# One scatter a unit instead of two, and folds kept out of the units that split rows

## The chip, the cores and the metric

The kernel runs on one core of a Trainium2 chip. The metric is the device time of one execution in microseconds (us). The engines are named as in the profile: PE is TensorE, DVE is VectorE, ACT is ScalarE, POOL is GpSimd, SP is SyncE, which here issues transfers. PEld is PE's loading of weights, which runs beside its products.

## The reference, cut to what matters

```python
X = np.fft.fft(np.fft.fft(x, axis=1), axis=2).real   # x: 8 x 3072 x 256
x = X.reshape(24576, 256)
x = (x @ w_a) * (x @ w_b) @ w_out                    # 256 -> 1536 -> 256
logits = x @ w_gate                                  # 8 experts
e_idx = argmax(logits)
gate_w = softmax(logits)[e_idx]
eom = sigmoid(x @ w_output_gate)
for e in range(8):                                   # tokens of expert e only
    out[mask] = gate_w * eom[e] * (relu(x[mask] @ w1[e]) @ w2[e])
```

## The kernel before, in words

Numbers are carried as pairs of fp16, a high and a low half, so one fp32 product becomes three fp16 ones. The program has two parts. In the first, up to about 1990 us, the transform, the first block of products and the gate are computed, and each token's row is written to an area of DRAM that is sorted by expert. In the second, the experts' products run over that area. The change touches the first part alone.

The first part is a list of 327 units (`plan`), which every engine runs through in the same order. A tile is 1024 tokens, 3 for each of the 8 batches (0 to 23), and takes 12 units, f 0 to 11. In each of them PE makes 12 products of 128x512 (line 828, into `s`) and 24 of 128x256 (line 894, into `y`), for one unit behind. Between them DVE makes five passes over `s` (lines 835 to 840 for the unit before, 861 for this one, into `EE`). The second half of PE's line 828 needs line 861's two results. Line 840 ends a unit's share on DVE; then ACT makes the high half of the result `hl` (line 845) and POOL the low half (line 847, "the subtraction" from here on). Units of a second kind, nine before tiles 6, 12 and 18, hold the transform's products.

Beside this chain every unit takes up pieces of other work, and a planner places them. `deal` goes through a list of items, each with a least distance to the one before and a cost for each engine, and moves an item to the next unit until the unit's `BUDGET` and a budget over three units (`THREE`) hold. A piece for "pool0" is put ahead of the unit's subtraction on POOL, one for "pool" or "dve" behind the unit's own work. The pieces that the change and the prediction speak of:

- `post_items(T)`, after a tile: squares, then the rows in two halves, on ACT (`row_hi`) and on DVE (`row_lo`, line 947, "low halves" from here on: 2, 3 and 3 of them in three units, which are f 4, 5 and 6 of the next tile), transposes issued by SP (`turn`), the gate (`gate0` to `gate3`), the place in the sorted area (`place`) and last eight scatters (line 1050), which POOL issues as indirect transfers and which each wait for the landing of the one before.
- `fold_items(b)`, for the batches ahead: six chunks c, each with a first piece (`fold1`, lines 519 to 521) and a second (`fold2`, lines 529 to 532, and for c of 3 to 5 lines 534 and 535 too), on POOL; SP loads and places rows beside them.
- `expert_items(e)`: the experts' weights are split into halves, the low ones on DVE (lines 412 and 465).

```python
t.append((1 + (i == 0 and k == 0), [("pool", 2.1 if k == 0 else 3.6 if c > 2 else 2.2, fn)] + nx + due))
```

Of the kernel before, what the change touches and what calls it, by code (L numbers as in the profile page):

```python
# [13 lines left out]
ALU = mybir.AluOpType  # L14
# [4 lines left out]
B, S, D = 8, 3072, 256  # L19
# [15 lines left out]
NTILE = 3 * B  # L35
# [6 lines left out]
def chain_kernel(ctx, tc, x, x384, w_a, w_b, w_out, w_gate, w_og, w1, w2, dft, c16, c32, ids, out):  # L42
    nc = tc.nc
    w_a, w_b, w_out = (w.bitcast(I32).rearrange("a (b c) -> a b c", c=2) for w in (w_a, w_b, w_out))
    pe, act, dve, pool, sp = nc.tensor, nc.scalar, nc.vector, nc.gpsimd, nc.sync
# [12 lines left out]
    def place_at(off, dtype, shape, spec, **kw):  # L58
        size = 4 if dtype in (FP32, I32) else 2
        n = 1  # L60
        for k in shape:
            n *= k
        v = big[:, off // 2:off // 2 + n * size // 2]
        if dtype != FP16:
            v = v.bitcast(dtype)
        return v.rearrange(spec, **kw) if spec else v
# [5 lines left out]
    F32 = place_at(24576, FP32, [6, 2, D], "p (a b c) -> p a b c", a=6, b=2)  # L72
# [99 lines left out]
    def run(point):  # L172
# [1 line left out]
            fn()  # L174

    BUDGET = {
        "B": {"act": 2.8, "dve": 1.75, "pool": 3.6, "pe": 1.0, "sp": 4.0},
        "D": {"act": 1.8, "dve": 1.8, "pool": 3.2, "pe": 1.0, "sp": 4.0},
    }
    THREE = {"act": 6.5, "dve": 5.0, "pool": 9.0}  # L180

# [316 lines left out]
    def fold_items(b, eng):  # L498
        st = {}
# [15 lines left out]
        def fold1(c):  # L515
            def go():
                P = st["P", c]
                Q = place_at(Qo, FP32, [4, D], "p (a b) -> p a b", a=4)
                eng.tensor_tensor(out=Q[:, :, 0:128], in0=P[:, :, 0:128], in1=P[:, :, 128:256], op=ALU.add)
                eng.tensor_tensor(out=Q[:, :, 129:256], in0=P[:, :, 0:127], in1=P[:, :, 128:255], op=ALU.subtract)  # L520
                eng.tensor_copy(out=Q[:, :, 128:129], in_=P[:, :, 256:257])
            return go

        def fold2(c):
            def go():
                P = st.pop(("P", c))
                Qv = place_at(Qo, FP32, [4, D], "p (h j d) -> p h j d", h=2, j=2)
                A, T = P[:, 0:2, 0:256], P[:, 2, 0:256]
                eng.tensor_tensor(out=A[:, :, 0:129], in0=Qv[:, :, 0, 0:129], in1=Qv[:, :, 1, 0:129], op=ALU.add)
                eng.tensor_tensor(out=A[:, :, 129:256], in0=Qv[:, :, 0, 129:256], in1=Qv[:, :, 1, 129:256], op=ALU.subtract)  # L530
                eng.tensor_tensor(out=T if c > 2 else F32[:, c, 0, :], in0=A[:, 0, :], in1=A[:, 1, :], op=ALU.add)
                eng.tensor_tensor(out=F32[:, c, 1, :], in0=A[:, 0, :], in1=A[:, 1, :], op=ALU.subtract)
                if c > 2:
                    eng.tensor_tensor(out=F32[:, c, 0, :], in0=F32[:, c - 3, 0, :], in1=T, op=ALU.subtract)
                    eng.tensor_tensor(out=F32[:, c - 3, 0, :], in0=F32[:, c - 3, 0, :], in1=T, op=ALU.add)
            return go

        def norm(c):
# [64 lines left out]
        t = [(0, [("sp", 1, load(0))])]  # L603
        norms = deque()
        for i, c in enumerate(order):
            for k, fn in enumerate((fold1(c), fold2(c))):
                if i == 1 and k == 0:
                    t.append((0, [("sp", 1, load384)]))
                due = [norms.popleft()] if i > 3 and norms else []
                nx = [("sp", 1, load(order[i + 1]))] if k == 1 and i < 5 else []  # L610
                t.append((1 + (i == 0 and k == 0), [("pool", 2.1 if k == 0 else 3.6 if c > 2 else 2.2, fn)] + nx + due))
            if i == 1:
                t.append((1, [("sp", 1, place384)]))
            if c > 2:
                norms += [("act", 0.6, norm(c - 3)), ("act", 0.6, norm(c))]
# [285 lines left out]
    def post_items(T):  # L901
        t, j0, nj = T
        ns = 1 if t == NTILE else 2
        nt = nj * ns
        st = {}
# [142 lines left out]
        def scatter(w):  # L1048
            def go():
                pool.indirect_dma_start(out=rows, out_offset=bass.IndirectOffsetOnAxis(ap=st["di"][:, w:w + 1], axis=0), in_=rowit[:, w, :], in_offset=None, bounds_check=ROWS - 1, oob_is_err=False)  # L1050
            return go

        def c(fn, a, b):
            return fn(min(a, nt), min(b, nt))

        k = nt / 8
        items = [
        ]
# [3 lines left out]
        last = None  # L1062
        for a, b in ((0, 2), (2, 5), (5, 8)):
            if a >= nt:
                continue
            m = min(b, nt) - a
            items.append((0 if last is None and nt > 4 else 1, [("act", 0.4 * m, c(row_hi, a, b)), ("dve", 0.38 * m, c(row_lo, a, b))] + ([("sp", 2, last)] if last else [])))
            last = c(turn, a, b)
        items += [
            (1, [("sp", 2, last), ("dve", 0.4, gate0)]),  # L1070
# [2 lines left out]
            (1, [("act", 0.25, exp2), ("dve", 0.8, gate3)]),  # L1073
            (0, [("pe", 1, place_pe), ("act", 0.25, place_copy), ("dve", 1.1, place)]),
        ]
        for w in range(0, nt, 2):
            items.append((1, [("pool0", 1.3, scatter(w))] + ([("pool", 1.3, scatter(w + 1))] if w + 1 < nt else [])))
        return items

# [134 lines left out]
    for u, un in enumerate(plan):  # L1214
        if un[0] == "D":
            first_of.setdefault(un[1], u)
            if pending:
                T, f = pending.pop(0)
                if f == NF - 1:
                    ends[T] = u  # L1220
        else:
            begins.setdefault(un[1], u)
            pending.append((un[1], un[2]))
            if len(pending) > 3:
                T, f = pending.pop(0)
# [28 lines left out]
    with tc.manual_schedule():  # L1254
# [167 lines left out]
        for T in tiles:  # L1422
            t, j0, _ = T
# [52 lines left out]
        items, late_early, weigh = early_items()  # L1476
# [8 lines left out]
        for u, un in enumerate(plan):  # L1485
            if un[0] == "D":
                _, g, i, k, n = un
# [363 lines left out]
```

## Time and profile before

| | |
|---|---|
| Median of three runs | 3059.37 us (3047.44 to 3063.09) |
| Profiled execution | 3057.12 us, of which the profile's span is 3055.4 us |
| PE | 2881.0 us busy, 94% of the span |
| DVE, POOL, ACT | 2209.5, 1335.7, 1315.1 us busy |
| Mean granted clock of PE | 0.976 |

PE's share is so high that time can be lost only where PE stands still or has the lower clock; the idle time of the other engines matters where PE waits for them.

### The profile page before, as it was taken

The numbers are of one execution on the slowest core, as the hardware profiler recorded it, in microseconds if no ns is written. First come the engines' busy times: TensorE is split into PE (matmuls) and PEld (weight loads), VectorE is DVE, ScalarE is ACT, GpSimd is POOL, SyncE is SP. The second block draws the span as 40 slices with busy tenths as digits, with TensorE's granted clock in tenths as the row PEclk, the third lists the DMA queues.
The fourth block names the chain that finished last, engine by engine and source line by source line (L and its number), as shares of the span: only waits on it lengthen the run. The fifth ranks groups of instructions, "written<-read, shape, count | busy, mean of one in ns | idle before, by whom it ended". The sixth has DMA issues, their size and how long they took to land.

```text
span 3055.4 us, 62396 instructions
## 1 busy us (share of the span) xinstructions
PE 2881.0 (94%) x24101; PEld 2184.9 (72%) x24101; DVE 2209.5 (72%) x4079; ACT 1315.1 (43%) x2605; POOL 1335.7 (44%) x1083
## 2 busy tenths in 40 slices
PE   6899899989999989999989999989999999999998
PEld 4466666656666756666666666678888888888898
DVE  8779699688999688999777998744555555555556
ACT  4454455545455445455444454432333333333332
POOL 6466587365775455775333445413211111111112
PEclk7899999999999999999999999999999999999999
DMA  5421722541221541221452212363222222222211
GB/s 190 118 60 43 177 74 60 145 107 40 77 76 47 137 116 46 77 72 46 99 126 84 77 50 82 87 186 98 58 51 51 50 53 52 51 53 51 51 44 35
DMA packets 363577, 244.48 MB, mean 80 GB/s; under 512 B 303101, under 2 KB 320669, under 8 KB 362382
## 3 DMA queue, kind: packets, MB, share of 16 engines
q1 hardware_dynamic: 342158, 184.75, 24.5%
q0 software_dynamic: 18816, 51.54, 4.9%
q10 hardware_dynamic: 2304, 4.20, 0.5%
q8 instruction: 188, 3.08, 0.4%
q14 instruction: 111, 0.91, 0.1%
HBM read 106.60 MB, written 70.33 MB: 58 GB/s over the span
## 4 chain that ended last, share of the span: by engine, by line
PE 75%; DVE 11%; issue 7%; DMA 3%; ACT 2%; POOL 0%; SPq 0%; DVEq 0%; POOLq 0%; ACTq 0%
PE s L828 19%; PE y L894 18%; PE g L1598 16%; PE g L1622 15%; PE s L662 3%; DVE EE L861 2%; DVE s L837 2%; DVE rows L947 1%; DVE hf L840 1%; DMA big<-in_dft_dram 1%; DVE AM L835 1%; DMA rows<-rows,di 1%; PE s L962 1%; ACT BP L834 1%; PE s L289 1%
## 5 line engine op out<-in xcount | busy, mean ns | idle before, releaser
L828 PE MATMUL s<-big 128*128 128x512 f16 x3456 | 824.9, 389 | 74.1 <-DVE EE L861 66.8
L847 POOL TENSOR_TENSOR hl<-hf,hl 128x1024 f16<-128x1024 f32 x288 | 626.4, 2175 | 566.2 <-ACT hl L845 422.9
L894 PE MATMUL y<-big,hl 128*128 128x256 f16 x6912 | 821.6, 273 | 1.0 <-POOL hl L847 1.0
L894 PEld LDWEIGHTS <-hl 128*128 128x128 f16 x6912 | 672.8, 98 | 152.0 <-issue 12.2
L828 PEld LDWEIGHTS <-big 128*128 128x128 f16 x3456 | 344.2, 100 | 448.4 <-issue 118.2
L1625 POOL DMA_INDIRECT out_dram<-o,di x189 | 195.4, 1034 | 777.3 <-ACT o L1624 524.8
L845 ACT ACTIVATE hl<-hf 128x1024 f16<-128x1024 f32 x288 | 303.8, 1055 | 499.2 <-DVE hf L840 434.3
L1598 PE MATMUL g<-yt,w1t 128*128 128x256 f16 (+1 forms) x4704 | 492.8, 265 | 3.5 <-DVE w1t L1579 3.5
L1622 PE MATMUL g<-w2t,hh 128*128 128x256 f16 x2896 | 479.5, 273 | 0.0
L1598 PEld LDWEIGHTS <-w1t 128*128 128x128 f16 x4704 | 432.0, 98 | 50.1 <-DVE w1t L1579 3.8
L1601 DVE SCALAR_TENSOR_TENSOR hl<-g,hh 128x512 f16<-128x512 f32 x378 | 260.3, 691 | 240.8 <-ACT hh L1600 239.9
L1622 PE MATMUL g<-w2t,hl 128*128 128x256 f16 x1448 | 394.7, 273 | 0.0
L1600 ACT ACTIVATE hh<-g 128x512 f16<-128x512 f32 x378 | 225.3, 598 | 276.3 <-PE g L1598 276.3
L1622 PEld LDWEIGHTS <-hh 128*128 128x128 f16 x3024 | 295.0, 98 | 33.7
L1050 POOL DMA_INDIRECT rows<-rows,di x192 | 191.7, 998 | 264.4 <-DMA rows<-rows,di 199.2
L836 DVE SCALAR_TENSOR_TENSOR hf<-s,BP 128x512 f32<-128x512 f32 x288 | 198.3, 688 | 112.9 <-ACT BP L834 102.7
L1583 DVE COPY w2t<-big 128x4104 f16 x98 | 120.5, 1229 | 206.7 <-PE g L1622 206.7
L1624 ACT ACTIVATE o<-g,sc 128x256 f32<-128x256 f32 x189 | 89.7, 474 | 409.6 <-PE g L1622 360.5
L835 DVE SCALAR_TENSOR_TENSOR AM<-EE,s 128x512 f32<-128x512 f32 x288 | 195.9, 680 | 30.7 <-PE s L828 28.3
L861 DVE SCALAR_TENSOR_TENSOR EE<-big,w,s 128x512 f32<-128x512 f32 x288 | 201.5, 741 | 0.0
L861 DVE SCALAR_TENSOR_TENSOR EE<-xe,w,s 128x512 f32<-128x512 f32 x288 | 201.4, 740 | 0.0
L834 ACT ACTIVATE BP<-s 128x512 f32<-128x512 f32 x288 | 170.2, 591 | 67.6 <-PE s L828 64.3
(332 smaller groups left out, 3039.5 us busy)
## 6 DMA issues: line engine op xcount, KB each, us to landing
big<-in_x_dram SPq DMA_DIRECT2D x48, 514.0 KB
big<-in_dft_dram SPq DMA_DIRECT2D x60, 384.0 KB
big<-in_moe_w_dram SPq DMA_DIRECT2D x16, 1024.0 KB
wsc<-big SPq DMA_DIRECT2D x32, 512.0 KB
big<-wsc SPq DMA_DIRECT2D x7, 2050.0 KB
big<-in_dft_dram SPq DMA_DIRECT2D x60, 192.0 KB
big<-wsc ACTq DMA_DIRECT2D x16, 256.2 KB
raw<-in_moe_w_out_dram SPq DMA_DIRECT2D x6, 512.0 KB
```

What stands on the lines that cost most here:

```text
L828: pe.matmul(out=s[ab], lhsT=Wt[:, ab, uv, a, fs], rhs=src[:, h + uv, :], start=(uv == 0 and i == 0), stop=(i == 2), skip_group_check=(uv = ...
L834: act.activation(out=BP, in_=b, func=ACTF.Copy)
L835: dve.scalar_tensor_tensor(out=AM[:, 0, :], in0=EE[:, 0, :], scalar=2.0, in1=a, op0=ALU.mult, op1=ALU.subtract)
L836: dve.scalar_tensor_tensor(out=P["hf"][:, 0, :], in0=a, scalar=CA * CA, in1=BP, op0=ALU.mult, op1=ALU.mult)
L845: act.activation(out=hl[:, 0], in_=hf, func=ACTF.Copy)
L847: pool.tensor_tensor(out=hl[:, 1], in0=hf, in1=hl[:, 0], op=ALU.subtract)
L861: dve.scalar_tensor_tensor(out=EE[:, ab, :], in0=st_x[T[0]], scalar=w0[:, ab, f:f + 1], in1=s[ab], op0=ALU.mult, op1=ALU.add)
L894: pe.matmul(out=Y[w // 2][:, w % 2, :], lhsT=hl[:, h, pm, 128 * j:128 * j + 128], rhs=wo[:, f, a, :], start=(f == 0 and i == 0 and w % 2 = ...
L1598: pe.matmul(out=ps[:, u, :], lhsT=w[:, a, q, 128 * f:128 * f + 128], rhs=yt[:, 2 * h + q, :], start=(m == 0), stop=(m == 5))
L1600: act.activation(out=hh[:, f0:f0 + nu, :], in_=ps, func=ACTF.Relu)
L1601: dve.scalar_tensor_tensor(out=hl[:, f0:f0 + nu, :], in0=ps, scalar=0.0, in1=hh[:, f0:f0 + nu, :], op0=ALU.max, op1=ALU.subtract)
L1622: pe.matmul(out=ps, lhsT=hx[:, f, ts], rhs=wv[:, a, f, :], start=(m == 0), stop=(m == 3 * NF2 - 1))
```

## The change

The eight scatters of tiles 6 to 19 are dealt one to a unit, all as "pool0", instead of two to a unit. A new resource, "lock", has a budget of 1.0 in each unit: an item of low halves takes 1.0 of it for tiles from 6 on, a piece of a fold takes 0.5 for batches from 4 on. So a unit has either low halves or at most two pieces of a fold. For batches from 4 on the last two instructions of a second piece (lines 534 and 535, now 539 and 540) become a piece of their own, `fold3`, which may stand in the unit of the second piece or later. No instruction is added or left out.

```diff
-        "B": {"act": 2.8, "dve": 1.75, "pool": 3.6, "pe": 1.0, "sp": 4.0},
+        "B": {"act": 2.8, "dve": 1.75, "pool": 3.6, "pe": 1.0, "sp": 4.0, "lock": 1.0},
...
+                st["T", c] = T
+            return go
+
+        def fold3(c):
+            def go():
+                T = st["T", c]
+                eng.tensor_tensor(out=F32[:, c, 0, :], in0=F32[:, c - 3, 0, :], in1=T, op=ALU.subtract)
+                eng.tensor_tensor(out=F32[:, c - 3, 0, :], in0=F32[:, c - 3, 0, :], in1=T, op=ALU.add)
+            return go
+
+        def both(c):
+            def go():
+                fold2(c)()
                 if c > 2:
-                    eng.tensor_tensor(out=F32[:, c, 0, :], in0=F32[:, c - 3, 0, :], in1=T, op=ALU.subtract)
-                    eng.tensor_tensor(out=F32[:, c - 3, 0, :], in0=F32[:, c - 3, 0, :], in1=T, op=ALU.add)
+                    fold3(c)()
...
-            for k, fn in enumerate((fold1(c), fold2(c))):
+            for k, fn in enumerate((fold1(c), both(c)) if b < 4 else (fold1(c), fold2(c)) + ((fold3(c),) if c > 2 else ())):
...
-                t.append((1 + (i == 0 and k == 0), [("pool", 2.1 if k == 0 else 3.6 if c > 2 else 2.2, fn)] + nx + due))
+                t.append((int(k < 2) + (i == 0 and k == 0), [("pool", (2.1, 2.2 if c < 3 or b > 3 else 3.6, 1.35)[k], fn), ("lock", 0.5 if b > 3 else 0.0, None)] + nx + due))
...
-            items.append((0 if last is None and nt > 4 else 1, [("act", 0.4 * m, c(row_hi, a, b)), ("dve", 0.38 * m, c(row_lo, a, b))] + ([("sp", 2, last)] if last else [])))
+            items.append((0 if last is None and nt > 4 else 1, [("act", 0.4 * m, c(row_hi, a, b)), ("dve", 0.38 * m, c(row_lo, a, b)), ("lock", 1.0 if t > 5 else 0.0, None)] + ([("sp", 2, last)] if last else [])))
...
-        for w in range(0, nt, 2):
+        if 5 < t < NTILE - 4:
+            items += [(1, [("pool0", 1.3, scatter(w))]) for w in range(nt)]
+        for w in range(0, nt if not 5 < t < NTILE - 4 else 0, 2):
             items.append((1, [("pool0", 1.3, scatter(w))] + ([("pool", 1.3, scatter(w + 1))] if w + 1 < nt else [])))
```

The first place is POOL in tile 11, f 0 to f 6, where nothing but subtractions (TENSOR_TENSOR hl) and the scatters of tile 9 (DMA rows) stands; the numbers behind a name are those of buffers and differ between the two kernels. Before:

```order
L847 TENSOR_TENSOR hl_10634<-hf_10590,hl_10634 128x1024
L1050 DMA rows_60<-rows2_100,di_10645 196864x264
L847 TENSOR_TENSOR hl_10694<-hf_10660,hl_10694 128x1024
L1050 DMA rows_60<-rows2_100,di_10645 196864x264 x2
L847 TENSOR_TENSOR hl_10753<-hf_10717,hl_10753 128x1024
L1050 DMA rows_60<-rows2_100,di_10645 196864x264 x2
L847 TENSOR_TENSOR hl_10814<-hf_10774,hl_10814 128x1024
L1050 DMA rows_60<-rows2_100,di_10645 196864x264 x2
L847 TENSOR_TENSOR hl_10874<-hf_10838,hl_10874 128x1024
L1050 DMA rows_60<-rows2_100,di_10645 196864x264
L847 TENSOR_TENSOR hl_10937<-hf_10902,hl_10937 128x1024
L847 TENSOR_TENSOR hl_10993<-hf_10958,hl_10993 128x1024
```

The same place now:

```order
L859 TENSOR_TENSOR hl_10626<-hf_10582,hl_10626 128x1024
L1062 DMA rows_60<-rows2_100,di_10637 196864x264
L859 TENSOR_TENSOR hl_10686<-hf_10652,hl_10686 128x1024
L1062 DMA rows_60<-rows2_100,di_10637 196864x264
L859 TENSOR_TENSOR hl_10742<-hf_10706,hl_10742 128x1024
L1062 DMA rows_60<-rows2_100,di_10637 196864x264
L859 TENSOR_TENSOR hl_10800<-hf_10760,hl_10800 128x1024
L1062 DMA rows_60<-rows2_100,di_10637 196864x264
L859 TENSOR_TENSOR hl_10857<-hf_10821,hl_10857 128x1024
L1062 DMA rows_60<-rows2_100,di_10637 196864x264
L859 TENSOR_TENSOR hl_10917<-hf_10882,hl_10917 128x1024
L1062 DMA rows_60<-rows2_100,di_10637 196864x264
```

Pairs of scatters stood back to back between two subtractions, and all eight were past by f 4. Now one stands ahead of each subtraction, and the eight reach to f 8, past the low halves of tile 10 in f 4 to f 6.

The second place is POOL in tile 14, f 5 to f 7 before and to f 8 now; `big` is written by the pieces of a fold. Low halves stand on DVE in f 5 and f 6. Before:

```order
L847 TENSOR_TENSOR hl_13803<-hf_13767,hl_13803 128x1024
L519 TENSOR_TENSOR big_63<-big_63 128x4x128
L520 TENSOR_TENSOR big_63<-big_63 128x4x127
L521 COPY big_63<-big_63 128x4
L847 TENSOR_TENSOR hl_13865<-hf_13830,hl_13865 128x1024
L529 TENSOR_TENSOR big_63<-big_63 128x2x129
L530 TENSOR_TENSOR big_63<-big_63 128x2x127
L531 TENSOR_TENSOR big_63<-big_63 128x256
L532 TENSOR_TENSOR big_63<-big_63 128x256
L847 TENSOR_TENSOR hl_13924<-hf_13891,hl_13924 128x1024
```

And now:

```order
L859 TENSOR_TENSOR hl_13791<-hf_13755,hl_13791 128x1024
L1062 DMA rows_60<-rows2_100,di_13495 196864x264
L859 TENSOR_TENSOR hl_13851<-hf_13816,hl_13851 128x1024
L1062 DMA rows_60<-rows2_100,di_13495 196864x264
L859 TENSOR_TENSOR hl_13909<-hf_13876,hl_13909 128x1024
L519 TENSOR_TENSOR big_63<-big_63 128x4x128
L520 TENSOR_TENSOR big_63<-big_63 128x4x127
L521 COPY big_63<-big_63 128x4
L1062 DMA rows_60<-rows2_100,di_13495 196864x264
L859 TENSOR_TENSOR hl_13971<-hf_13938,hl_13971 128x1024
```

The first two pieces of the fold of batch 7 move from f 5 and f 6 to f 7 and f 8, behind the low halves, and scatters take their place. In f 8 two low halves of an expert's weights (line 465) stand on DVE in both kernels.

The third place is POOL at the end of tile 8 and the start of tile 9 (f 10, f 11 and f 0), where DVE makes `gate2`, `gate3` and `place`. Before:

```order
L847 TENSOR_TENSOR hl_8984<-hf_8950,hl_8984 128x1024
L529 TENSOR_TENSOR big_63<-big_63 128x2x129
L530 TENSOR_TENSOR big_63<-big_63 128x2x127
L531 TENSOR_TENSOR big_63<-big_63 128x256
L532 TENSOR_TENSOR big_63<-big_63 128x256
L847 TENSOR_TENSOR hl_9055<-hf_9010,hl_9055 128x1024
```

And now:

```order
L859 TENSOR_TENSOR hl_8974<-hf_8938,hl_8974 128x1024
L529 TENSOR_TENSOR big_63<-big_63 128x2x129
L530 TENSOR_TENSOR big_63<-big_63 128x2x127
L531 TENSOR_TENSOR big_63<-big_63 128x256
L532 TENSOR_TENSOR big_63<-big_63 128x256
L539 TENSOR_TENSOR big_63<-big_63 128x256
L540 TENSOR_TENSOR big_63<-big_63 128x256
L859 TENSOR_TENSOR hl_9047<-hf_9004,hl_9047 128x1024
```

Here the fold of batch 5 runs one chunk behind its place of before, so that a second piece with its end stands in f 11, ahead of the unit with `place`.

## Rows read from the trace of the kernel before

**Rows 1.** The page: busy time by engine, then two groups (busy, mean ns | idle).

```profile
PE 2881.0 (94%) x24101; PEld 2184.9 (72%) x24101; DVE 2209.5 (72%) x4079; ACT 1315.1 (43%) x2605; POOL 1335.7 (44%) x1083
...
L828 PE MATMUL s<-big 128*128 128x512 f16 x3456 | 824.9, 389 | 74.1 <-DVE EE L861 66.8
...
L894 PE MATMUL y<-big,hl 128*128 128x256 f16 x6912 | 821.6, 273 | 1.0 <-POOL hl L847 1.0
```

**Rows 2.** Waits of the whole span: us in total, times, longest.

```profile
POOL rows L1050 <- DMA rows<-rows,di: 199.2, 82, 6.0
...
PE s L828 <- DVE EE L861: 66.8, 34, 6.1
```

**Rows 3.** Windows, tile 7: length, each engine's busy time, granted clock, DMA.

```profile
688.80:753.30 64.50, 64.50 (x485) 43.63 (x484) 54.99 (x111) 37.40 (x75) 36.96 (x28) 1.00 0.16 41
```

**Rows 4.** Windows, tiles 8 to 11, 14 to 17, 20 and 21; sum of all ten.

```profile
753.30:826.30 73.00, 66.91 (x495) 44.41 (x494) 67.96 (x122) 34.85 (x65) 50.14 (x40) 0.95 0.28 81
...
1762.50:1832.40 69.90, 67.14 (x496) 44.54 (x495) 64.01 (x125) 34.25 (x62) 34.09 (x20) 0.98 0.19 54
sum 698.10, PE 662.31 PEld 442.48 DVE 638.58 ACT 351.70 POOL 418.38; mean PE 66.23 PEld 44.25 DVE 63.86 ACT 35.17 POOL 41.84
```

**Rows 5.** Timeline of DVE in tile 7 (start us, us; xN merged).

```profile
713.07 0.68 DVE L840 SCALAR_TENSOR_TENSOR hf<-s,AM 128x512 f32<-128x512 f32 x1
...
718.28 0.68 DVE L840 SCALAR_TENSOR_TENSOR hf<-s,AM 128x512 f32<-128x512 f32 x1
718.88 1.27 DVE L947 SCALAR_TENSOR_TENSOR rows<-tail,r,rows 128x256 f16<-128x256 f32 x3
```

**Rows 6.** Timeline of POOL in tile 7.

```profile
714.98 2.13 POOL L847 TENSOR_TENSOR hl<-hf,hl 128x1024 f16<-128x1024 f32 x1 [2.85 <-ACT hl L845]
720.20 2.14 POOL L847 TENSOR_TENSOR hl<-hf,hl 128x1024 f16<-128x1024 f32 x1 [3.09 <-ACT hl L845]
```

**Rows 7.** Timeline of DVE in tile 10.

```profile
919.89 0.69 DVE L840 SCALAR_TENSOR_TENSOR hf<-s,AM 128x512 f32<-128x512 f32 x1
...
926.21 5.03 DVE L947 SCALAR_TENSOR_TENSOR rows<-tail,r,rows 128x256 f16<-128x256 f32 x3
...
936.72 0.74 DVE L465 SCALAR_TENSOR_TENSOR big<-big,r2e 128x512 f16<-128x512 f32 x1
```

**Rows 8.** Timeline of POOL in tile 10.

```profile
924.49 0.97 POOL L1050 DMA_INDIRECT rows<-rows,di  x1 [1.80 <-DMA rows<-rows,di]
925.48 2.15 POOL L847 TENSOR_TENSOR hl<-hf,hl 128x1024 f16<-128x1024 f32 x1
927.79 1.00 POOL L1050 DMA_INDIRECT rows<-rows,di  x1 [0.16 <-issue]
928.80 2.15 POOL L847 TENSOR_TENSOR hl<-hf,hl 128x1024 f16<-128x1024 f32 x1
936.84 2.61 POOL L847 TENSOR_TENSOR hl<-hf,hl 128x1024 f16<-128x1024 f32 x1 [5.89 <-ACT hl L845]
```

**Rows 9.** Line 947 from 926 to 932 us: ns min/median/max, first and last start.

```profile
L947 DVE SCALAR_TENSOR_TENSOR rows<-tail,r,rows x3: 474/1702/3008, 926.2 to 928.2; 128x256 f16<-128x256 f32 x3
```

**Rows 10.** Windows of POOL alone, a first piece and a full second piece.

```profile
637.80:640.50 2.70, 2.63 (x4) 0.83 0.82 218
702.80:707.00 4.20, 3.96 (x8) 1.00 0.01 2
```

**Rows 11.** Timeline of PE in tile 8.

```profile
783.65 2.75 PE L828 MATMUL s<-big 128*128 128x512 f16 x12
786.24 2.78 PE L894 MATMUL y<-big,hl 128*128 128x256 f16 x24
795.11 4.72 PE L828 MATMUL s<-big 128*128 128x512 f16 x12 [6.09 <-DVE EE L861]
```

**Rows 12.** Timeline of DVE in tile 6, two low halves of weights.

```profile
675.45 3.24 DVE L412 SCALAR_TENSOR_TENSOR big<-big,r1e 128x512 f16<-128x512 f32 x2
```

**Rows 13.** DMA issues: median us from issue to landing.

```profile
rows<-rows,di POOLq DMA_INDIRECT x192, 2.5
```

**Rows 14.** Waits of SP's queue, whole span.

```profile
SPq L556 <- POOL big L535: 47.4, 5, 14.1
```

More of the change, by code (lines that the diff above doesn't have):

```diff
@@ L176, in chain_kernel @@
     BUDGET = {
-        "B": {"act": 2.8, "dve": 1.75, "pool": 3.6, "pe": 1.0, "sp": 4.0},
-        "D": {"act": 1.8, "dve": 1.8, "pool": 3.2, "pe": 1.0, "sp": 4.0},
+        "B": {"act": 2.8, "dve": 1.75, "pool": 3.6, "pe": 1.0, "sp": 4.0, "lock": 1.0},
+        "D": {"act": 1.8, "dve": 1.8, "pool": 3.2, "pe": 1.0, "sp": 4.0, "lock": 1.0},
     }
```

## The prediction

> **What bounds the kernel now.** The page comes first: PE is busy for 94% of the span, so only PE's standstills and its clock are to be had. Its two largest groups say where it stands. The products of line 894, which need POOL's subtraction, wait 1.0 us in the whole run; those of line 828 wait 74.1 us, 66.8 of them for DVE's `EE` [rows 1]. So POOL being late costs PE nothing by itself, and DVE being late costs it directly. The list of waits says the same: 34 waits for `EE`, the longest 6.1 us [rows 2].
>
> Which units are these? Tile 7 takes 64.5 us with PE busy throughout [rows 3]. Ten tiles that differ from it only in what lies beside the chain (8 to 11, 14 to 17, 20, 21) take 698.1 us together, and PE is busy for 662.3 of them [rows 4]. The timelines of DVE and POOL show the difference. In tile 7, line 840 starts at 713.07 and at 718.28, so a unit lasts 5.21 us. The three low halves follow from 718.88 to 720.15 [rows 5]. POOL's subtraction of that unit starts at 720.20, when ACT has made its input, 1.92 us after line 840 started; the one before ended at 717.11, 1.77 us before the low halves began [rows 6]. The two engines pass each other, and no scatter is near: those of tile 6 come in tile 8.
>
> In tile 10 the same three low halves take 5.03 us instead of 1.27 [rows 7]. POOL is late there. Line 840 started at 919.89, so its subtraction was due at 921.81; it starts at 925.48, 3.7 us late, behind a scatter that waited 1.80 us for the landing of the one before [rows 8]. Such waits add up to 199.2 us in 82 cases [rows 2], and eight scatters in four units have no room for them. The late subtraction runs over the start of the low halves, a last scatter and the next subtraction follow back to back, and the low halves take 474, 1702 and 3008 ns [rows 9]. The third starts at 928.2, inside the scatter, and ends with the subtraction behind it, at 931.2. So a low half, which reads two arrays from SBUF, stands still while a subtraction runs that does the same. DVE runs in order, the passes over `s` queue behind the low half, and PE waits for them.
>
> **The change part by part.** *Removed: the hits in the ten tiles.* Against ten times tile 7 they lose 698.1 − 645.0 = 53.1 us. Standstill is 698.1 − 662.3 = 35.8 of it. The other 17.3 is busy time: 108 more matmuls (4958 in the ten windows' counts against 4850), narrow ones such as the nine of `place`, and PE's lower clock after a long wait. For the clock: the 12 products of a unit take 2.75 us, but 4.72 behind a wait of 6.09, and tile 8's granted clock is 0.95 in the mean [rows 11, 4]. That is near half the rate for a few products, the lower of PE's two levels (1.2 instead of 2.4 GHz). For the 108 matmuls I take 0.05 us each, 5 us, an estimate between 0 and 2.78/24 = 0.12 us, the step of a product of 128x256 [rows 11]. So 48 us are there to be had, 41 to 53 by these ends.
>
> Does the change take the cause away? A unit now costs POOL one subtraction (2.14 us) and one scatter (1.0), 3.1 of 5.21 us, and the next scatter comes a unit later, while a landing takes 2.5 us from issue in the median [rows 6, 8, 13]. The scatter fits in the 3.09 us in which POOL was idle. So the subtraction comes when ACT releases it, as in tile 7, though a scatter now stands in every unit with low halves. Where pieces of a fold stand too, 3.1 us and 2.63 for a first piece (2.6 to 4.0 by kind) [rows 10] are 5.8 us, 0.6 more than a unit; two such units in a row make POOL 1.2 us late, less than the 1.77 that the low halves leave, and the lock keeps the next units free. I take all 48 us as removed.
>
> *Added: weight splits behind low halves.* Eight pairs of units hold an item of low halves and a split (0.74 us) on DVE. Three low halves alone cost nothing in tile 7, and the split gets ahead of the subtraction by 0.12 us (936.72 against 936.84, the subtraction then takes 2.61 instead of 2.14) [rows 7, 8]. DVE is then behind by a part of 0.74 us. Between 0 and 16 times 0.74 = 11.8, I take 2.5 us, near tile 7.
>
> *Added: folds at new places.* A first or second piece starts behind its subtraction and ends in the next unit, where other operations with two SBUF inputs may stand. I count five places where that is new or gets longer: `place` in tile 9 f 0, two splits in tile 14 f 8 and in tile 12 f 10, `gate3` in tile 6 f 4, splits in f 8 of tiles 9 and 15 (half a place each). The nearest price: two splits took 3.24 us instead of 1.4 where a subtraction was in the way [rows 12], so 1.8 each, 9 us; the ends are 0 and five full hits of 3.01 − 0.47 = 2.5 [rows 9], 12.7.
>
> *Moved at no cost.* The scatters end four units later; their rows are read in the second part only. SP's loads and placings go with the pieces. The placing of batch 4 (SP) now stands two units earlier, in a stretch of the transform, and waits for POOL's fold there; what queues behind it are transposes and a load of transform tables. Waits of this kind are there already, 47.4 us in five cases, up to 14.1 [rows 14], without PE showing them. So 0, and 3 us if that load becomes late. In the transform's stretches before tiles 12 and 18 there are no subtractions, so a low half meets a scatter alone: 0.
>
> The sum: 3057.1 − 48 + 2.5 + 9 = 3020.6, made against the profiled execution (span 3055.4 and 1.7 around it), which is 2.3 us below the median of the three runs. I predict **3021 us**. The ends of the terms give 3057.1 − 53 = 3004 and 3057.1 − 41 + 11.8 + 12.7 + 3 = 3044.
>
> **A rule beside the rows.** The third low half of tile 10 was on its engine 0.6 us before the subtraction started, and still ran after it [rows 8, 9]. The Trainium skill says otherwise (SBUF — State Buffer, Who interferes with whom): a DVE instruction with two SBUF inputs contends with a GpSimd instruction that reads SBUF, descriptor generation is inferred not to, and issue order decides who blocks. By that the low half would have gone first, in 0.47 us. The row disagrees: a subtraction that is queued behind a scatter already shuts the low half out. The sum stays by either, since the 48 us are measured; by the rule alone the slower rival below would have no price.
>
> **The rivals.** *The scatter comes late among the low halves (slower).* Tiles 8 to 11, 14 to 17, 20 and 21 now have a scatter in each of three units with low halves. If POOL is over 1.77 us late there, each unit takes a hit of 2.5 us [rows 9]. All 30 would cost 76 us: 3057 + 76 − 37 = 3096. It decides from 15 hits on, as 15 × 2.5 = 37. For it: landings can keep POOL waiting 6.0 us [rows 2]. Against it: a scatter that follows a unit later has 4.2 us for its landing, and the subtractions leave POOL 2 us a unit to catch up.
>
> *Half the gain is eaten.* If nearly every piece of a fold that ends in a next unit with a split, a low half of a batch or a gate meets it fully, some seven further hits of 2.5 us come to the five: 3021 + 18 = 3039. For it: in tile 6 the gate and the splits are hit today without low halves in the way [rows 12]. Against it: gate operations stand where PE works at logits.
>
> *No change.* If the low halves are late by themselves, DVE being full, nothing is won: 3057. Against it stands tile 7, with the same low halves and no wait [rows 3, 5].
>
> **How the numbers follow.** Forecast (3004 to 3031) 0.68; half the gain (3031 to 3044) 0.15; no change 0.09; slower 0.08. The range 3002 to 3043 holds the first two but for the edges, 0.81. A change of 0.5% is 15 us, as wide as the three runs before lie apart and about what a measurement of this kernel can tell from none; below 3042 is "faster": 0.81, same 0.11, slower 0.08.
>
> **What would show it.** In the windows of tiles 8, 14 and 16 lengths near 65 to 68 us instead of 70 to 73, with a clock near 1.0. PE's wait for `EE` falls from 66.8 us to about 35. POOL's waits for landings fall well below 199.2 us. Line 947's maxima near 0.5 us in tiles 8 to 17. Tiles 22 and 23, whose scatters stay in pairs, keep their hits. I am wrong if line 947 still has cases of 3 us in f 4 to f 6 (the scatters come late), if line 465 or 412 has cases over 2 us at f 5 to f 8, or if the wait for `EE` is replaced by one for another tile.

## The result, and the profile after

The changed kernel takes 3008.92 us in the median of four runs (3002.82 to 3013.22); the kernel before took 3054.07 in the median of four beside it. The ratio is 0.985, with a 95% interval of 0.981 to 0.989. The profiled execution took 3006.51 us, 3004.7 of them its span, so 50.7 us less than before.

The page of the changed kernel: busy time by engine, then the two groups of [rows 1] under their new lines (840 for 828, 906 for 894).

```profile
PE 2858.8 (95%) x24101; PEld 2179.2 (73%) x24101; DVE 2161.1 (72%) x4079; ACT 1316.3 (44%) x2605; POOL 1337.1 (44%) x1083
...
L840 PE MATMUL s<-big 128*128 128x512 f16 x3456 | 806.4, 383 | 46.6 <-DVE EE L873 37.7
...
L906 PE MATMUL y<-big,hl 128*128 128x256 f16 x6912 | 819.7, 273 | 1.1 <-POOL hl L859 1.1
```

Its list of waits (us in total, times, longest), for [rows 2]:

```profile
POOL rows L1062 <- DMA rows<-rows,di: 139.2, 53, 5.6
...
PE s L840 <- DVE EE L873: 37.7, 25, 3.8
```

PE's wait for `EE` fell from 66.8 to 37.7 us, POOL's waits for landings from 199.2 to 139.2. DVE is busy 48.4 us less with the same 4079 instructions, 41.3 us of it in the low halves and 4.8 in the weights' splits: that was time in which an instruction was recorded as busy and stood still.

The windows of tiles 8, 14 and 21 and the sum of the ten tiles of [rows 4] (columns as in [rows 3]):

```profile
751.20:815.80 64.60, 64.60 (x493) 43.72 (x492) 58.70 (x116) 35.47 (x65) 42.95 (x31) 1.00 0.28 83
...
1193.90:1259.80 65.90, 64.97 (x495) 43.84 (x494) 62.41 (x118) 33.77 (x65) 46.38 (x35) 1.00 0.29 81
...
1713.20:1779.00 65.80, 65.35 (x496) 44.07 (x495) 60.71 (x125) 34.08 (x62) 34.40 (x20) 1.00 0.20 57
sum 652.10, PE 649.46 PEld 439.36 DVE 597.76 ACT 351.20 POOL 418.81; mean PE 64.95 PEld 43.94 DVE 59.78 ACT 35.12 POOL 41.88
```

The ten tiles take 652.1 instead of 698.1 us, at a granted clock of 1.00. PE's standstill in them fell from 35.8 to 2.6 us.

The timelines of POOL and DVE at the low halves of tile 10, for [rows 7, 8]:

```profile
906.76 1.00 POOL L1062 DMA_INDIRECT rows<-rows,di  x1 [0.17 <-issue]
908.59 2.13 POOL L859 TENSOR_TENSOR hl<-hf,hl 128x1024 f16<-128x1024 f32 x1 [0.84 <-ACT hl L857]
910.88 1.00 POOL L1062 DMA_INDIRECT rows<-rows,di  x1 [0.16 <-issue]
913.81 2.60 POOL L859 TENSOR_TENSOR hl<-hf,hl 128x1024 f16<-128x1024 f32 x1 [1.93 <-ACT hl L857]
```

```profile
911.88 0.69 DVE L852 SCALAR_TENSOR_TENSOR hf<-s,AM 128x512 f32<-128x512 f32 x1
912.48 1.27 DVE L959 SCALAR_TENSOR_TENSOR rows<-tail,r,rows 128x256 f16<-128x256 f32 x3
913.67 0.75 DVE L465 SCALAR_TENSOR_TENSOR big<-big,r2e 128x512 f16<-128x512 f32 x1
```

The subtraction waits for ACT again, 1.93 us after line 852 (line 840 of before) started, and the three low halves take 1.27 us instead of 5.03. Line 959 (947 of before) by duration, ns min/median/max, first in tiles 8 to 11, then in tiles 22 and 23, whose scatters stay in pairs:

```profile
L959 DVE SCALAR_TENSOR_TENSOR rows<-tail,r,rows x32: 475/480/486, 776.6 to 983.3; 128x256 f16<-128x256 f32 x32
```

```profile
L959 DVE SCALAR_TENSOR_TENSOR rows<-tail,r,rows x16: 469/477/3012, 1805.1 to 1888.9; 128x256 f16<-128x256 f32 x16
```

### The profile page after: what moved, and what is told of

Its sections match the earlier page's. It is cut to its first block, busy times and chain, and to the rows that moved or that the text cites. A ratio compares the mean times of both kernels' runs of the same rounds, so it can differ in the third digit from the quotient of the medians.

```text
span 3004.7 us, 62398 instructions
## 1 busy us (share of the span) xinstructions
PE 2858.8 (95%) x24101; PEld 2179.2 (73%) x24101; DVE 2161.1 (72%) x4079; ACT 1316.3 (44%) x2605; POOL 1337.1 (44%) x1083
## 4 chain that ended last, share of the span: by engine, by line
PE 80%; DVE 9%; issue 4%; DMA 3%; ACT 2%; POOL 0%; SPq 0%; DVEq 0%; POOLq 0%; ACTq 0%
PE y L906 21%; PE s L840 20%; PE g L1612 16%; PE g L1636 16%; PE s L674 3%; DVE EE L873 1%; DVE s L849 1%; DMA big<-in_dft_dram 1%; DVE hf L852 1%; PE s L974 1%; DVE AM L847 1%; DMA rows<-rows,di 1%; DVE rows L959 1%; PE s L289 1%; ACT big L702 1%
## 5 line engine op out<-in xcount | busy, mean ns | idle before, releaser
L840 PE MATMUL s<-big 128*128 128x512 f16 x3456 | 806.4, 383 | 46.6 <-DVE EE L873 37.7
L840 PEld LDWEIGHTS <-big 128*128 128x128 f16 x3456 | 340.1, 99 | 407.1 <-issue 68.3
L1062 POOL DMA_INDIRECT rows<-rows,di x192 | 192.9, 1005 | 196.6 <-DMA rows<-rows,di 139.2
L849 DVE SCALAR_TENSOR_TENSOR s<-EE,s 128x512 f32<-128x512 f32 x288 | 197.3, 685 | 0.0
```

What stands on the lines that cost most here:

```text
L840: pe.matmul(out=s[ab], lhsT=Wt[:, ab, uv, a, fs], rhs=src[:, h + uv, :], start=(uv == 0 and i == 0), stop=(i == 2), skip_group_check=(uv = ...
L849: dve.scalar_tensor_tensor(out=b, in0=EE[:, 1, :], scalar=2.0, in1=b, op0=ALU.mult, op1=ALU.subtract)
```

## The experiments

Each was timed against the kernel before. This table has the medians (the kernel before had 3054.1 beside the changed kernel, 3055.7 beside the next four, 3057.2 or 3057.3 beside the others) and, from the traces, the ten tiles' lengths in us (from the first of PE's products into `s` to that of the next tile; tiles 11 and 17 to f 11).

| | median (ratio, 95%) | 8 | 9 | 10 | 11 | 14 | 15 | 16 | 17 | 20 | 21 | sum |
|---|---|---|---|---|---|---|---|---|---|---|---|---|
| before | 3054.1 to 3057.2 | 73.0 | 68.6 | 70.5 | 60.7 | 72.8 | 70.3 | 70.3 | 61.9 | 69.7 | 69.9 | 687.6 |
| changed | 3008.9 (0.981–0.989) | 64.6 | 65.5 | 65.7 | 58.8 | 65.9 | 65.5 | 66.1 | 58.8 | 65.3 | 65.8 | 641.8 |
| scatters alone | 3015.7 (0.985–0.989) | 67.9 | 66.1 | 67.0 | 58.9 | 65.0 | 69.7 | 67.0 | 58.9 | 65.3 | 65.8 | 651.5 |
| lock alone | 3060.1 (0.998–1.002) | 71.2 | 67.9 | 73.0 | 61.0 | 69.4 | 72.8 | 72.0 | 62.3 | 70.1 | 71.6 | 691.3 |
| pairs later | 3058.8 (0.999–1.003) | 68.5 | 74.8 | 64.9 | 58.8 | 68.9 | 73.6 | 66.0 | 58.8 | 66.0 | 70.3 | 670.5 |
| one input | 3028.8 (0.989–0.993) | 73.5 | 68.3 | 68.2 | 58.8 | 71.0 | 69.6 | 70.0 | 58.8 | 69.9 | 67.9 | 675.8 |
| reduction | 2992.6 (0.977–0.981) | 68.6 | 66.9 | 64.9 | 58.8 | 65.0 | 68.6 | 65.3 | 58.8 | 65.3 | 66.6 | 648.7 |
| not split | 3011.6 (0.983–0.987) | 65.7 | 66.1 | 67.0 | 58.9 | 65.1 | 66.9 | 67.0 | 58.9 | 65.3 | 65.8 | 646.7 |

**Scatters alone: the kernel before with this edit.**

```diff
+        if 5 < t < NTILE - 4:
+            items += [(1, [("pool0", 1.3, scatter(w))]) for w in range(nt)]
-        for w in range(0, nt, 2):
+        for w in range(0, nt if not 5 < t < NTILE - 4 else 0, 2):
```

> The kernel before with one scatter a unit for tiles 6 to 19, without the lock and without the split of the fold's second piece. Theory (pairs of scatters make POOL late, and a late subtraction shuts out the low halves): the six tiles without folds in f 4 to f 6 (10, 11, 16, 17, 20, 21) come to the lengths they have in the changed kernel, which is 22.7 us less; tiles 9 and 14, where the planner now puts no fold beside low halves either, give 10 more; tile 15 part of its 4.8; tile 8 keeps folds in f 4 and f 5 and gives 0 to 8; tile 13 gets two pieces of a fold beside low halves, a loss of 0 to 5. Sum: a median of 3015 to 3028 us. Rival (the lock brings the gain, because it keeps folds away from low halves): 3045 to 3057 us, with tiles 10, 16 and 20 still over 69 us.

Measured: 3015.7 us, in the theory's range. The tiles without a fold fall to their lengths of the changed kernel within 1.4 us. Tile 8 keeps 3.3 us, tile 15 4.2, where a piece of a fold still stands beside low halves. In tile 13, where the expectation had a loss of 0 to 5 us, nothing is lost (64.5 us in both).

**Lock alone: the changed kernel with scatters in pairs again** (the same lines, taken back; the split second piece stays).

> The changed kernel with scatters back in pairs; lock and split second piece stay. Theory of the pairs: tiles 10, 11, 16, 17, 20 and 21 keep their lengths of before, since no fold stood beside their low halves; tiles 8, 9, 14 and 15 lose the fold beside the low halves but still have a pair in f 4, and fall to about 70 us, the length of tile 10, which is 3.0 + 0 + 2.8 + 0 = 6 us less. A median of 3043 to 3055 us. Rival (the lock brings the gain): 3009 to 3025 us, and line 959 has no case over 1 us in tiles 8 to 17.

Measured: 3060.1 us, no gain. Line 959 in tiles 8 to 11 shows why: the long cases are there as before, with the folds gone.

```profile
L959 DVE SCALAR_TENSOR_TENSOR rows<-tail,r,rows x32: 464/478/3015, 782.6 to 1007.5; 128x256 f16<-128x256 f32 x32
```

So the lock, with the split, is worth something only once POOL is on time: 641.8 against the 651.5 us of the scatters alone in the ten tiles. The intervals of the two medians overlap; the tiles' lengths are what shows it.

**Pairs later: the kernel before with the pairs behind the low halves.**

```diff
-            items.append((1, [("pool0", 1.3, scatter(w))] + ([("pool", 1.3, scatter(w + 1))] if w + 1 < nt else [])))
+            items.append((7 if w == 0 and 5 < t < NTILE - 4 else 1, [("pool0", 1.3, scatter(w))] + ([("pool", 1.3, scatter(w + 1))] if w + 1 < nt else [])))
```

> The kernel before with the scatters still in pairs, but from the seventh unit after the place on (f 7 to f 10 instead of f 1 to f 4), so behind the low halves; no lock, no split. Theory (only POOL's lateness at the low halves counts): tiles 10, 11, 16, 17, 20 and 21, which then have no scatter and no fold at f 4 to f 6, fall to 64 to 67 us although each still has four pairs; gates and splits of f 7 to f 10 may be hit by up to 2 us a tile; tiles 8, 9, 14 and 15 have folds beside low halves, but no scatter there, and keep a part of their loss. A median of 3015 to 3040 us. Rival (pairs of scatters cost by themselves, wherever they stand, by the waits for landings): these six tiles stay near 69 us and the median at 3045 to 3065.

Measured: 3058.8 us, a miss for the sum. Five of the six tiles did what the theory says (64.9, 58.8, 66.0, 58.8 and 66.0 us, with four pairs in each). The loss came back where the pairs and the folds they push went: tile 9 6.2 us longer than before, tile 13 6.8, tile 15 3.3, the stretch of the transform before tile 12 8.4 (its cause was not followed). In tile 13 pairs now stand ahead of the low halves, and the first two of these meet what those of f 5 met in tile 10 of before. DVE, then POOL:

```profile
1181.51 3.47 DVE L947 SCALAR_TENSOR_TENSOR rows<-tail,r,rows 128x256 f16<-128x256 f32 x2
```

```profile
1181.53 0.99 POOL L1050 DMA_INDIRECT rows<-rows,di  x1 [0.17 <-issue]
1182.54 2.15 POOL L847 TENSOR_TENSOR hl<-hf,hl 128x1024 f16<-128x1024 f32 x1
```

Tile 21 is the sixth: late subtractions run over the first operation of `place` at 1764.98, which takes 3.77 us. So pairs do no harm at low halves that they don't reach; they make POOL late for the operation with two arrays that comes next, low halves in tile 13 and `place` in tile 21.

**One input: the kernel before, the low half as a scaling of one array.**

```diff
-                    dve.scalar_tensor_tensor(out=rowt[:, w, 256:512], in0=Yt[:, w, :], scalar=st["r"][:, w:w + 1], in1=rowt[:, w, 0:256], op0=ALU.mult, op1=ALU.subtract)
+                    dve.tensor_scalar(out=rowt[:, w, 256:512], in0=Yt[:, w, :], scalar1=st["r"][:, w:w + 1], scalar2=None, op0=ALU.mult)
```

> The kernel before with scatters in pairs, where the low half of a row is made by an operation that reads one array instead of two: the scaled row itself is stored in place of the rest that the high half leaves, so the gate's values and the outputs are not the reference's. Theory (a low half stands still because it reads two arrays from SBUF while the subtraction, which does the same, runs or is next on POOL): with one array no low half is over 0.8 us anywhere, also in tiles 22 and 23 and before tile 6, and the median falls to 2995 to 3020 us, although POOL is as late as before. Rival (the low half waits for something else, or DVE is late because its queue is full): the cases of 1.7 to 3 us stay and the median is within 15 us of before.

Measured: 3028.8 us, between the two. Line 947 from 640 us on (ns min/median/max), then DVE and POOL in tile 10:

```profile
L947 DVE TENSOR_SCALAR rows<-tail,r x144: 334/347/2233, 709.8 to 1967.3; 128x256 f16<-128x256 f32 x144
```

```profile
921.15 2.74 DVE L947 TENSOR_SCALAR rows<-tail,r 128x256 f16<-128x256 f32 x3
923.80 3.21 DVE L465 SCALAR_TENSOR_TENSOR big<-big,r2e 128x512 f16<-128x512 f32 x1
```

```profile
920.98 2.15 POOL L847 TENSOR_TENSOR hl<-hf,hl 128x1024 f16<-128x1024 f32 x1
923.30 0.99 POOL L1050 DMA_INDIRECT rows<-rows,di  x1 [0.17 <-PE s L828]
924.30 2.15 POOL L847 TENSOR_TENSOR hl<-hf,hl 128x1024 f16<-128x1024 f32 x1
```

The theory as I put it, that two inputs are what counts, falls: this operation has one, and one of them still stood until the subtraction had ended (923.13). The second hit moved on to the weight split behind it, so in tiles with a split there (8, 10, 14, 16, 20, 21) a split takes 3.2 to 5.8 us and the tile stays at 67.9 us or more. Tiles 9 and 15, where pieces of a fold stand, stay long too; tiles 11 and 17 come free. What stands out is that one takes 347 ns in the median, where the form with two inputs takes 480. The Trainium skill (VectorE: DVE Perf Modes, Mode 2×_2P — use both read ports for one tensor) says that such an operation reads its one array through both read ports when array and result lie in SBUF, as here, and (SBUF — State Buffer, Who interferes with whom) that it contends with GpSimd for that reason, while a reduction on this chip never does.

**Reduction: the kernel before, with this in place of the same line.**

```diff
+                    dve.tensor_reduce(out=rowt[:, w, 256:512], in_=rowt[:, w, 0:256].unsqueeze(2), axis=AX.X, op=ALU.max)
```

> The kernel before with scatters in pairs, where the low half of a row is made by a reduction over an axis of length one, which copies the high half: one array is read, at one element a step; the gate's values and the outputs are not the reference's. In the run with the scaling operation of one input, the low halves took 349 ns instead of 474 alone, and still stood still until a running subtraction ended (2187 ns at 1379.75 us). Theory A (that operation was faster because it reads its one array through both ways into SBUF, and so was shut out like one with two inputs; an operation that reads one array in one way is free): no low half over 0.7 us anywhere; tiles 11, 17, 22 and 23, which have no weight split in f 5 and f 6 but one, lose nothing at the low halves; in tiles 8, 10, 14, 16 and 20 the split behind them may still be hit once; median 3000 to 3030 us. Theory B (any DVE operation on SBUF waits while a subtraction runs): low halves of 1 to 3 us stay, median 3025 to 3060 us.

Measured: 2992.6 us, theory A, below its range. Line 947 from 640 us on, then DVE and POOL in tile 10:

```profile
L947 DVE TENSOR_REDUCE rows<-rows x144: 399/409/421, 700.7 to 1925.5; 128x256 f16<-128x256 f16 x144
```

```profile
906.17 1.06 DVE L947 TENSOR_REDUCE rows<-rows 128x256 f16<-128x256 f16 x3
907.15 1.47 DVE L465 SCALAR_TENSOR_TENSOR big<-big,r2e 128x512 f16<-128x512 f32 x1
```

```profile
905.91 2.15 POOL L847 TENSOR_TENSOR hl<-hf,hl 128x1024 f16<-128x1024 f32 x1
```

Three low halves run through in the middle of a subtraction, and the split behind them, with two inputs, waits for its end. POOL is as late as before (the subtraction starts 0.3 us ahead of the low halves and is still running at their end), and the kernel is 64.6 us faster. Over the whole run 47 of these low halves start inside a subtraction, and none is held. With the scaling of one array 14 of 15 were held, with the form of two arrays 96 of 101 (all ten profiled runs that keep it). These counts agree with the two sections of the Trainium skill that are named above; the ports themselves are in no trace.

**Twice: the changed kernel with each scatter issued twice in its unit.**

```diff
-            items += [(1, [("pool0", 1.3, scatter(w))]) for w in range(nt)]
+            items += [(1, [("pool0", 1.3, scatter(w)), ("pool0", 0.0, scatter(w))]) for w in range(nt)]
```

> The changed kernel, where each of the scatters of tiles 6 to 19 is issued twice in its unit (the same rows to the same places, so a second scatter that waits for the landing of the first stands ahead of each subtraction). Theory (what decides is whether POOL is on time at the low halves): a unit now costs POOL 2.14 + 2 x 1.0 + about 1.5 us of waiting for the landing = 5.6 of 5.21 us, so POOL falls behind by 0.4 us a unit or more from f 1 on and is over the margin of 1.77 us at f 4 to f 6; at least two of the three units with low halves in ten tiles take a hit of 2.5 us each, 20 to 30 hits: 50 to 75 us over the changed kernel, 3058 to 3085 us. Rival (what counted was the fold beside the low halves, POOL's lateness by scatters does no harm): 3009 to 3025 us.

Measured: 3186.3 us (ratio 1.043, 1.041 to 1.046), far over the range, which left out that PE would wait for the subtraction itself. PE's waits:

```profile
PE y L906 <- POOL hl L859: 85.5, 46, 11.6
PE s L840 <- DVE EE L873: 65.8, 48, 3.7
```

The wait for `EE` grew by 28 us, but POOL, whose scatters, landings and subtraction now take more than a unit, became a bound by itself: PE waits 85.5 us for `hl`, 1.1 in the changed kernel. The two waits grew by 112 us together, of the 172 by which the profiled executions differ; the rest was not followed.

**A dose: only the fourth scatter, in f 4 of the ten tiles, twice or three times.**

```diff
+            items += [(1, [("pool0", 1.3, scatter(w))] + [("pool0", 0.0, scatter(w))] * (1 if w == 3 else 0)) for w in range(nt)]
```

> The changed kernel, where of the eight scatters of tiles 6 to 19 only the fourth, which in ten tiles stands in f 4 ahead of the subtraction, is issued twice (the same rows to the same places). A test of the margin of 1.77 us: counted from line 840 of f 4, the first of the two starts at -1.15, lands at 1.35, the second runs from 1.35 to 2.35, so the subtraction, due at 1.92, is 0.43 us late. Theory of the margin: below 1.77 us nothing happens at the low halves of f 5 and f 6, and the median is that of the changed kernel, 3005 to 3014 us. Rival (any lateness of POOL costs, in proportion): 0.4 to 1 us in each of ten tiles and more where a scatter is active at the low halves of f 4, 3015 to 3030 us.

> As the run with the fourth scatter twice, but three times: the third waits for the second landing at 3.85 us after line 840 and ends at 4.85, so the subtraction of f 4 is 2.9 us late and runs to 7.0, over the start of the low halves of f 5 at 5.8. Theory of the margin: above 1.77 us the first low half of f 5 waits for the end of the subtraction (1.2 us), a later one meets the next scatter with a ready subtraction behind it (2.5 us), as in tile 10 of before: 3 to 5 us in each of ten tiles, 3035 to 3060 us, and line 959 has cases of 3.0 us in f 5 of tiles 8 to 11. Rival (proportion): about seven times the lateness of the run before this one, but only as much as POOL's own delay reaches the products of y; with no hit in line 959, 3010 to 3025 us.

Measured: 3021.7 us (ratio 0.987 to 0.993) and 3061.8 (1.000 to 1.003), outside the theory's ranges by 8 and 2 us; the first lies in the range of the rival (its profiled execution, which the tiles below come from, took 3015.9 us). The tiles tell them apart. Below is how late the subtraction of f 4 starts (its start, less that of line 852 in f 4, less 1.92) and what the tile takes more than in the changed kernel, both in us:

| tile | 8 | 9 | 10 | 11 | 14 | 15 | 16 | 17 | 20 | 21 |
|---|---|---|---|---|---|---|---|---|---|---|
| twice: late | 0.95 | 2.22 | 1.89 | 0.93 | 1.02 | 4.20 | 1.69 | 1.10 | 1.05 | 0.97 |
| twice: longer | 0.0 | 2.1 | 0.0 | 0.0 | 0.0 | 5.8 | −0.4 | 0.0 | 0.0 | 0.0 |
| three times: late | 4.09 | 5.26 | 5.24 | 4.15 | 5.64 | 5.28 | 5.14 | 3.91 | 3.89 | 3.86 |
| three times: longer | 6.6 | 2.2 | 2.2 | 5.1 | 2.5 | 2.2 | 1.9 | 3.2 | 5.5 | 5.5 |

In the changed kernel it is at most 0.26 us late, in the kernel before 2.5 to 4.7. Up to 1.89 us nothing is lost, from 2.22 on each tile pays: a limit, and not the rival's proportion, since the tiles that are 5 us late pay less than those that are 4 us late. Tile 8 of the run with two, DVE and POOL, shows a lateness that costs nothing (779.76 − 776.90 − 1.92 = 0.94):

```profile
776.90 0.68 DVE L852 SCALAR_TENSOR_TENSOR hf<-s,AM 128x512 f32<-128x512 f32 x1
```

```profile
778.77 0.98 POOL L1062 DMA_INDIRECT rows<-rows,di  x1 [1.74 <-DMA rows<-rows,di]
779.76 2.15 POOL L859 TENSOR_TENSOR hl<-hf,hl 128x1024 f16<-128x1024 f32 x1
```

Tiles 9 and 15 went over since POOL was late by 1.3 and 3.1 us in f 3 already, by pieces of a fold in f 1 and f 2 and in tile 15 by a landing that a scatter waited 2.1 us for. In tile 9 it is the split behind the low halves that waits (alone 0.75 us):

```profile
849.65 2.88 DVE L412 SCALAR_TENSOR_TENSOR big<-big,r1e 128x512 f16<-128x512 f32 x1
```

These two tiles, and 2.8 us in tile 12, where a low half of the transform's stretch met a first piece of a fold (2.07 us at 1060.76), are where the estimate of the run with two was short. In the run with three, tile 8 takes both hits:

```profile
787.91 5.96 DVE L959 SCALAR_TENSOR_TENSOR rows<-tail,r,rows 128x256 f16<-128x256 f32 x3
```

So do tiles 11, 17, 20 and 21. The others are 5.1 to 5.6 us late: there the low halves take one hit of 3.0 us, in tile 14 none but a split of 3.3, and PE also waits 0.7 to 1.1 us for the subtraction itself. So what the prediction read from the kernel before, that POOL being late costs PE nothing by itself, no longer holds at 5 us.

**Not split: the changed kernel with the second piece of a fold in one.** 

```diff
-            for k, fn in enumerate((fold1(c), both(c)) if b < 4 else (fold1(c), fold2(c)) + ((fold3(c),) if c > 2 else ())):
+            for k, fn in enumerate((fold1(c), both(c))):
```

> The changed kernel without the split of the fold's second piece: lines 529 to 532 and the last two instructions are one piece again, with the cost of before. Theory (scatters give the gain, the lock a small rest, the split nothing of its own): 3006 to 3018 us. Rival (the split is needed, since a whole second piece of 4 us makes POOL late in the next unit): 3020 us or more, with the loss in tiles 8, 9, 14 and 15.

Measured: 3011.6 us. The ten tiles are 4.9 us longer than in the changed kernel and 4.8 shorter than with the scatters alone, so there the split is worth as much as the lock, and neither much; the intervals of the medians overlap.

**More: one scatter a unit and the lock from tile 3 to tile 21.**

```diff
-("lock", 1.0 if t > 5 else 0.0, None)
+("lock", 1.0 if t > 2 else 0.0, None)
...
-        if 5 < t < NTILE - 4:
+        if 2 < t < NTILE - 2:
...
-                early_at = v
+                early_at = v - 4
```

> The changed kernel with one scatter a unit and the lock for tiles 3 to 21 instead of 6 to 19 (lock for all from 3 on), and the first choice of rows for the second part placed as early as before. Theory: tiles 22 and 23, which keep hits of 2.5 us in the changed kernel, come to about 65.3 and 60.5 us (from 69.0 and 63.8), 7 us; tile 6 comes to tile 12's 74.7 (from 78.9), 4 us; tile 5 gives 1 to 4; the stretch behind tile 5 may lose or win 1. A median of 2993 to 3003 us. Rival (later scatters of the last tiles keep the second part waiting): the gain in tiles 22 and 23 comes back as a wait at the start of the second part, and the median is 3003 to 3015 us.

Measured: 2992.2 us (ratio 0.979, 0.976 to 0.981), below the whole range of the changed kernel's runs. From 640 to 1917 us no low half is late any more, and PE waits 26.2 us for `EE` in the whole run:

```profile
L959 DVE SCALAR_TENSOR_TENSOR rows<-tail,r,rows x136: 472/479/486, 705.1 to 1875.1; 128x256 f16<-128x256 f32 x136
```

Tiles 22 and 23 give 4.3 and 4.2 us, tile 5 4.9, tile 6 3.7, tiles 8 and 12 lose 1.3 and 2.2, and nothing came back at the second part. This is the fastest version that computes what the reference does.

## Why the prediction was right, point by point

**Removed.** 48 us were forecast in the ten tiles; 46.0 came, net of new losses (below): 33.2 of the 35.8 us of standstill, and 12.8 us of PE's busy time (662.3 to 649.5), where 12.3 were counted for the clock. About the 5 us for narrow matmuls stayed, as they should: 649.5 − 645.0 = 4.5. The cause was put down right as to place (POOL late at the low halves; dose and reduction) and limit (1.77 us; the dose puts it between 1.89 and 2.22). It was too narrow in one word: two inputs are not what counts, since a scaling of one array is held too and a reduction of one array is not. None of the signs that the prediction named against itself showed: no low half of tiles 8 to 17 takes over 0.49 us, no split of f 5 to f 8 over 1.52, and no other wait of PE took the place of that for `EE`.

**Splits behind low halves.** Forecast 2.5, measured 0.6 at most. In tile 10 the split stands at 913.67, the subtraction at 913.81 takes 2.60, and the unit 5.21; only tile 16 (0.4) and tile 20 (0.2) have longer units behind a split.

**Folds at new places.** Forecast 9, measured about 4, and not where it was counted; this is the term that was mis-sized. None of the units of the five places is longer than before. Splits wait in tile 14 f 8 (1.51 us instead of 0.74), and in tiles 9 and 15 f 8, where they take 1.51 against 1.76 before; in tile 12 f 10 and at `gate3` in tile 6 the long wait is gone. The price of 1.8 us was taken from tile 6, where splits wait in full for a subtraction; here each waited 0.8 us for a piece of a fold, and that was in hand. Tile 14 f 8, the two splits on DVE:

```profile
1240.39 2.18 DVE L465 SCALAR_TENSOR_TENSOR big<-big,r2e 128x512 f16<-128x512 f32 x2
```

What was paid came at places that the sum did not count: small operations of the gate and of `place` wait for a piece of a fold and so come to stand in the subtraction behind it. It is 1.1 us in tile 14 f 11 (`gate2`), 0.8 each in tiles 10 and 16 f 1 (`place`), and in tile 6 2.7 in f 6 (`place`), with 1.6 won in f 5. The longest of them in tiles 14 and 10 (alone about 0.2 us):

```profile
1253.17 2.18 DVE L1013 TENSOR_TENSOR go<-ohx,L 128x64 f32<-128x64 f16 x1
```

```profile
887.01 1.72 DVE L1058 TENSOR_TENSOR di<-df 128x8 int32<-128x8 f32 x1
```

**Moved at no cost.** The transform's stretch before tile 12 was put at 0, as there are no subtractions in it. But there were pieces of a fold: two groups of three low halves at its end took 4.09 and 1.98 us before, over such pieces, and 1.28 and 1.27 now. Tile 12 f 0 takes 7.19 instead of 10.51 us. The lock does not do this: with the lock alone the longest of the six still takes 2.98 us and f 0 11.40, with the scatters alone none is held and f 0 takes 7.74. Together with 1.8 us in f 10 and f 11, tile 12 gives 4.4 us, which the sum didn't hold.

The profiled execution has 3006.51 us, 50.7 less than before: 46.0 in the ten tiles and so 4.7 outside them. Tile 12 is the largest part of these; the other stretches differ by up to 4 us either way, which one execution of each kernel can't tell from chance. 3020.6 was forecast, so the sum was 14 us too high: 5 by the folds, 2 by the splits, 1 by the removed hits, and 6 by what was won outside the ten tiles. All four erred to the same side, so the measured time lies near the fast end of the range.

**The rivals.** The slower one had its point right: over the limit a hit of 2.5 us follows (run with three, 3061.8 us). It didn't come since POOL was on time at the low halves. "Half the gain is eaten" named what did happen at the gates and at `place`, but it cost about 4 us and not 27. "No change" fell with the ten tiles.

## What to carry to other kernels

A wait that an engine can afford may still cost another one time: look for where it is when the other has an operation that it can hold up, not at its own idle time. Pieces with a fixed latency behind them (here a scatter's landing) go one to a unit, and operations that can shut each other out get a common budget in the planner. A forecast of what collisions at new places will cost should be made from how much of a wait the waiting engine has in hand, not from the longest such wait in the trace, and should count the small operations too: here those of the gate and of `place` paid, and the large ones did not.

## What the runs showed of the hardware that was not expected

When a subtraction stands behind a scatter, the prediction said that it shuts a low half out as soon as it is queued. The rule is sharper. In the ten profiled runs that keep the two-input low half (before, changed and eight variants) 205 low halves and splits start inside a scatter that has a subtraction next. 75 of them start at most 0.69 us before the subtraction's start on record, with ACT's input already made: all 75 stand still until it ends. 19 start as close to it, but before ACT has released it: none is held. 66 start 0.75 us or more ahead with the subtraction released, 45 as far ahead without: none is held, and a low half of 0.47 us is done in time. So a subtraction that is ready acts as if it had the way into SBUF about 0.7 us before its recorded start, inside the scatter's record. By the Trainium skill (SBUF — State Buffer, Who interferes with whom) issue order decides who blocks; the recorded starts are not that order here, and no run shows when the subtraction was issued. The prediction's word that the row disagrees with this rule was too strong.

A low half that comes 0.57 us ahead takes 3.01 us, that wait, the subtraction's 2.15 and 0.3 at the end. As it needs 0.47 us alone, it is let go about 0.2 us before the subtraction's end on record: of the 101 low halves that start inside a subtraction, the 96 with 0.4 us of it or more to come are held, the five with 0.17 us or less are not. This puts the limit at about 1.97 us instead of 1.77, between the 1.89 and 2.22 of the dose. Where a split came first, it is the subtraction that takes 2.60 instead of 2.14. A scatter by itself held none of the 130 others.
